# Layer 1's weight words bounded in a PSUM bank: clamp and shift there, the sign set before the add, the transposes moved into the scores' bank

## The chip, the cores and the metric

The kernel runs on one core of a Trainium2 chip. The metric is device time in microseconds (us) for one execution of the whole program, the median of three runs. One further execution is profiled: its trace gives the start and duration of the instructions on each engine. The engines are TensorE (PE in the rows), VectorE (DVE), ScalarE (ACT), GpSimd (POOL) and SyncE (SP, which issues the DMAs here).

## What is computed

Sparse attention feeds two feed-forward layers. All three parts are fp32.

```python
# attention: q, k, v are (4, 8, 576, 64); heads 0-3 local mask, heads 4-7 strided mask (stride 32)
scores = scale * np.matmul(q, k.transpose(0, 1, 3, 2))
scores = np.where(masks[None], scores, -1e9)
attn = np.exp(scores - np.max(scores, axis=-1, keepdims=True))
attn = attn / (np.sum(attn, axis=-1, keepdims=True) + 1e-09)
x = np.matmul(attn, v)                       # -> (2304 tokens, 512)
# layer 1: w_in (512, 2048), w_out (2048, 512)
h = x @ w_in
x = (h - np.tanh(h)) @ w_out
# layer 2: w_gate, w_val (512, 1536), w_out (1536, 512)
g = x @ w_gate
out = (g * (1.0 / (1.0 + np.exp(-g))) * (x @ w_val)) @ w_out
```

## The kernel before

TensorE multiplies in a split form: every fp32 operand is held as two reduced-precision halves, a head and a rest, and a product is three matmuls (head by head, head by rest, rest by head; `mm3`, L252 to L254).

The weights arrive as 64-bit words, and each must be turned into such a pair of halves. A `Piece` is 128 x 512 of them. Its steps are: `load` (a DMA into a slot `st` with a low and a high 32-bit word of each weight); `high` (ScalarE, the magnitude of the high word into `m`, L161); `low` (ScalarE, the low word scaled down, L164); the bounding of `m`, a clamp between two limits and a shift left and right that re-bases the exponent (VectorE); `join` (GpSimd, L189, adds the low word to `m`); `sign` (VectorE, L193, sets the sign bit of the high word into `m`); `head` (ScalarE, L199, the first half into `w`) and `rest` (GpSimd, L202, the second half).

Layer 1 has 32 such pieces, two for each slice `f` of 128 hidden columns. In the kernel before, `bound` does the clamp and the shift as two `scalar_tensor_tensor` instructions on `m` in place (L178 and L182). Their second input is a broadcast of a limit which lies in two spare columns of a PSUM bank (`limits`). One piece has the word `rebase` in its place: the two `tensor_scalar` forms of `clamp` and `shift` (L167 and L171), which work in SBUF alone. Layer 2's 36 pieces use `clamp`, `shift`, `join` and `sign` throughout.

Attention runs in groups of three blocks of scores. Its steps for a group are `scores` (TensorE, L344 or L352), `top` (VectorE, L360: mask, store to `s`, and the maximum of a row, three custom instructions with a read of the accumulator each), `exp` (ScalarE, L369), `recip` (VectorE, L382), `mult` (GpSimd, L387), `turn` (TensorE, L403: three transposes of `s` into PSUM), `bring` (VectorE, L407: a copy of them to SBUF as `pt`), `value` (TensorE, L415) and `keep` (ScalarE, L425, out of PSUM).

Two PSUM banks are set aside for this, `banks[0]` and `banks[1]`. Of `banks[0]` the scores take the first 288 columns and the values the rest; the transposes take 384 columns of `banks[1]`. The remaining banks hold the sums of layer 1.

What sets the order. There is no reordering on the chip: every engine takes its instructions in the order in which the program issues them. The first stretch, to about 60 us, is a text, `BEGIN`, that `Opening.run` reads word by word: `piece.3.bound` calls `bound` of piece 3, `turn.9` the transposes of group 9, `less.0`, `gh.0` and `gl.0` the three steps between the two products of layer 1's slice 0 (h - tanh h on VectorE, L824; the head on ScalarE, L828; the rest on VectorE, L833), `first` and `second` stretches of the two products (L798 and L811). After it a loop over `f` from 5 to 15 finishes the first chunk of 512 tokens. An iteration `f` there holds: the first product (12 matmuls, L252 to L254); `tanh` and `less` (ScalarE L608, VectorE L609; the function `bend`); the values of group f - 3 and the scores of group f; a `tick` of the weight feed; `top` of group f; the second product for f - 1 (12 matmuls, L628); `turn` and `bring` of group f - 1; the head and rest of f (ScalarE L615, VectorE L616; `parts`); `exp`, `recip`, `mult` of group f; and a second `tick`. Groups of this chunk end with group 16, and those of the loop then belong to the next batch. A tick issues `high` and `low` of one piece, `bound` and `join` of the piece before it and `sign`, `head` and `rest` of the one before that. Later chunks and layer 2 use no step of the change.

Of the kernel before, what the change touches and what calls it, by code (L numbers as in the profile page):

```python
# [70 lines left out]
piece.0.join piece.0.sign exp.7.c value.3 recip.6 piece.1.high mult.5.P low.2 turn.5 warm.12 keep.3 piece.1.low  # L71
bring.5.V words.2 ready.99.2 recip.7 top.8 exp.8.n mult.7.P warm.6 piece.1.bound value.4 keep.4 turn.7 keys.0.3
queries.0.3 mult.6.P bring.7.V turn.6 value.5 recip.8 piece.1.join piece.1.sign piece.0.head piece.2.high keep.5
scores.10 values.0.2 scores.9 scores.11 bring.6.V value.6 mult.8.P high.3 piece.0.rest ready.8.6 turn.8 low.3
piece.1.head words.3 xh.6 piece.1.rest top.9 top.10 exp.10.n values.0.3 xl.6 value.7 piece.2.bound words.4 words.5
keys.1.0 recip.10 top.11 ready.9.6 exp.9.c recip.9 mult.9.P xh.7 xl.7 piece.3.high mult.10.P ready.11.2 part.0.2
part.0.3 bring.8.V exp.11.c piece.3.low part.1.2 piece.3.bound recip.11 value.8 xh.8 left.8 xl.8 turn.9 turn.10
bring.9.V mult.11.A bring.10.V part.1.3 piece.3.join queries.1.0 value.9 values.1.0 keys.1.1 piece.2.low queries.1.1
piece.2.join xh.9 piece.4.high turn.11 piece.3.sign piece.3.head xl.9 part.0.0 bring.11.V value.10 value.11
piece.5.high xh.10 xh.11 piece.4.bound part.1.0 values.1.1 xl.11 left.11 first.3.2.1 xl.10 piece.4.low piece.5.low  # L80
words.6 scores.12 piece.2.sign piece.2.head piece.3.rest piece.5.bound half.0.0 half.0.1 words.7 piece.4.join tanh.0
top.12 piece.2.rest half.1.0 less.0 scores.13 half.1.1 first.3.2.11 piece.4.sign exp.12.c top.13 gh.0 gl.0
piece.5.join exp.13.c scores.14 second.2.0.8 tanh.1 piece.5.sign piece.5.head recip.12 recip.13 tanh.2 words.8 words.9
# [1675 lines left out]
```

## Time and profile before

| | |
|---|---|
| median of 3 runs | 865.82 us (865.76 to 866.29) |
| profiled execution | 866.21 us, of which the span of the trace is 864.4 us |
| granted TensorE clock | 1.00 throughout |
| TensorE busy | 859.2 us, 99% of the span |
| VectorE busy | 639.5 us, 74% |
| ScalarE busy | 463.8 us, 54% |
| GpSimd busy | 335.1 us, 39% |

The trace has a row for each instruction or run of equal instructions: start, duration, engine, source line, operation, output and inputs. Matmuls overlap in the pipeline, so that the durations of neighbours on TensorE add up to more than the time between them; distances between starts are what counts there. VectorE, too, starts an instruction some 0.1 us before the one ahead is recorded as ended. From the page's slices, VectorE is busy for over 90% of the time from about 22 to 130 us, where the weights of layer 1 are prepared, and less in most of the rest.

### The profile page before, as it was taken

To read this page: it belongs to the slowest core of one execution; us is meant where nothing else is said; L and a number is where in the kernel's file an instruction comes from. 1 tells how busy PE (TensorE), PEld (TensorE's weight loads), DVE (VectorE), ACT (ScalarE), POOL (GpSimd) and SP (SyncE) were. 2 spreads that over 40 slices of the span, in tenths; PEclk is the share of its full clock that TensorE was granted. 3 is DMA by queue.
4 is the path that set the end of the run, shared out by engine and by line. 5 is a ranking of instruction groups with operands and counts; after the bars stand their busy time and mean duration, and the time that the engine had idled before them with its cause. 6 is when DMAs were issued, how large, how long until landed. Compare 5 with 4: busy or idle time off the path is not lost.

```text
span 864.4 us, 13937 instructions
## 1 busy us (share of the span) xinstructions
PE 859.2 (99%) x4791; PEld 721.1 (83%) x4791; DVE 639.5 (74%) x1219; ACT 463.8 (54%) x1059; POOL 335.1 (39%) x284
## 2 busy tenths in 40 slices
PE   9999999999999999999999999999999999999998
PEld 7877778888888889998888888888888888888887
DVE  6999996688867786247887887788777867785461
ACT  6988874534343524237644655655454446854531
POOL 3889994754546550004125214463553310000000
PEclk9999999999999999999999999999999999999999
DMA  9867646530452213247456436453445469978651
GB/s 278 285 233 243 198 164 206 208 98 25 129 191 89 75 50 122 98 151 248 138 171 216 149 120 198 146 196 140 163 160 170 160 202 313 369 239 288 194 190 43
DMA packets 67398, 152.49 MB, mean 176 GB/s; under 512 B 7616, under 2 KB 14400, under 8 KB 67328
## 3 DMA queue, kind: packets, MB, share of 16 engines
q1 hardware_dynamic: 66752, 151.19, 52.2%
q8 instruction: 38, 0.62, 0.3%
q10 hardware_dynamic: 576, 0.41, 0.2%
q14 instruction: 32, 0.26, 0.1%
HBM read 108.06 MB, written 43.52 MB: 175 GB/s over the span
## 4 chain that ended last, share of the span: by engine, by line
PE 91%; DVE 4%; ACT 3%; issue 1%; DMA 0%; POOL 0%; SPq 0%; POOLq 0%
PE ps_acc L628 18%; PE ps_h L253 8%; PE ps_h L252 8%; PE ps_h L254 8%; PE ps_acc L252 8%; PE ps_acc L254 8%; PE ps_acc L253 8%; PE ps_a L252 5%; PE ps_a L253 5%; PE ps_a L254 5%; DVE m L193 2%; PE ps_acc L1628 2%; PE ps_a L415 1%; PE ps_a L344 1%; ACT s L369 1%
## 5 line engine op out<-in xcount | busy, mean ns | idle before, releaser
L628 PE MATMUL ps_acc<-gh,w 128*128 128x512 f32 (+1 forms) x546 | 124.8, 370 | 0.0
L189 POOL TENSOR_TENSOR sl<-sl,st 128x512 int32<-128x512 int32 x36 | 51.5, 1436 | 165.0 <-DVE sl L171 139.8
L252 PE MATMUL ps_acc<-sl 128*128 128x512 f32 x288 | 112.1, 389 | 0.0
L253 PE MATMUL ps_acc<-sl 128*128 128x512 f32 x288 | 112.1, 389 | 0.0
L254 PE MATMUL ps_acc<-sl 128*128 128x512 f32 x288 | 112.0, 389 | 0.0
L628 PEld LDWEIGHTS ps_acc<-gh,w 128*128 128x128 f32 x546 | 94.1, 189 | 16.1
L1214 DVE TENSOR_TENSOR sl<-sl 128x512 fp32r<-128x512 f32 (+1 forms) x120 | 71.8, 660 | 22.9 <-ACT sl L1210 22.8
L252 PE MATMUL ps_h<-xh,w 128*128 128x512 f32 (+1 forms) x226 | 85.0, 376 | 0.0
L253 PE MATMUL ps_h<-xh,w 128*128 128x512 f32 (+1 forms) x226 | 84.5, 374 | 0.1
L254 PE MATMUL ps_h<-xl,w 128*128 128x512 f32 (+1 forms) x226 | 84.2, 372 | 0.0
L1210 ACT CAST sl<-sl 128x512 fp32r<-128x512 f32 (+1 forms) x120 | 66.3, 602 | 24.7 <-DMA sl<-gd 18.8
L608 ACT ACTIVATE t<-ps_h 128x512 f32<-128x512 f32 (+1 forms) x54 | 30.5, 564 | 82.8 <-PE ps_h L254 82.8
L467 POOL TENSOR_TENSOR pr<-skv,sq 128x576 f32<-128x576 f32 (+8 forms) x40 | 57.5, 1463 | 44.4 <-DVE sc L474 31.1
L628 PE MATMUL ps_acc<-gl,w 128*128 128x512 f32 (+1 forms) x273 | 67.1, 366 | 0.0
L609 DVE TENSOR_TENSOR ps_h<-ps_h,t 128x512 f32<-128x512 f32 (+1 forms) x54 | 35.5, 658 | 41.0 <-ACT t L608 40.7
L254 PEld LDWEIGHTS ps_acc<-sl 128*128 128x128 f32 x288 | 54.1, 188 | 11.3
L252 PEld LDWEIGHTS ps_acc<-sl 128*128 128x128 f32 x288 | 54.1, 188 | 11.1
L253 PEld LDWEIGHTS ps_acc<-sl 128*128 128x128 f32 x288 | 54.1, 188 | 11.0
L467 POOL TENSOR_TENSOR pr<-skv,sc 128x576 f32<-128x576 f32 (+8 forms) x40 | 45.9, 1164 | 37.7 <-DVE xo L474 28.1
L252 PE MATMUL ps_a<-sl 128*128 128x512 f32 x144 | 56.1, 390 | 0.0
L253 PE MATMUL ps_a<-sl 128*128 128x512 f32 x144 | 56.1, 390 | 0.0
L254 PE MATMUL ps_a<-sl 128*128 128x512 f32 x144 | 56.0, 389 | 0.0
(211 smaller groups left out, 2098.4 us busy)
## 6 DMA issues: line engine op xcount, KB each, us to landing
st<-in_w SPq DMA_DIRECT2D x68, 512.0 KB, 4.4
gd<-t SPq DMA_DIRECT2D x84, 256.0 KB, 2.2
sl<-gd SPq DMA_DIRECT2D x84, 256.0 KB, 4.9
w<-w1s SPq DMA_DIRECT2D x32, 512.0 KB, 3.5
w3s<-sl SPq DMA_DIRECT2D x24, 256.0 KB, 3.3
sl<-w3s SPq DMA_DIRECT2D x24, 256.0 KB, 5.3
x2d<-o SPq DMA_DIRECT2D x17, 256.0 KB, 2.7
w1s<-w SPq DMA_DIRECT2D x8, 512.0 KB, 5.3
```

Of the source, the lines that this page charges most:

```text
L189: nc.gpsimd.tensor_tensor(out=mi, in0=mi, in1=self.lo, op=ALU.add)
L193: nc.vector.scalar_tensor_tensor(out=mi, in0=self.hi, scalar=-2 ** 30, in1=mi, op0=ALU.bitwise_and, op1=ALU.bitwise_or,)
L252: nc.tensor.matmul(ps, lhsT=wh, rhs=xh, start=start, stop=False, skip_group_check=goes_on)
L253: nc.tensor.matmul(ps, lhsT=wl, rhs=xh, start=False, stop=False, skip_group_check=goes_on)
L254: nc.tensor.matmul(ps, lhsT=wh, rhs=xl, start=False, stop=stop, skip_group_check=goes_on)
L467: nc.gpsimd.tensor_tensor(out=t, in0=x, in1=y, op=ALU.mult)
L608: nc.scalar.activation(t[:, :n], ps[:, :n], AF.Tanh)
L609: nc.vector.tensor_tensor(out=ps[:, :n], in0=ps[:, :n], in1=t[:, :n], op=ALU.subtract)
L628: nc.tensor.matmul(acc[m][:, :n], lhsT=w[:, i, m * P:(m + 1) * P], rhs=(gl if low else gh)[:, :n], start=start and not low and i == 0, sto ...
L1210: nc.scalar.copy(got[0][:, 0, :n], got[0][:, 1, :n].bitcast(F32))
L1214: nc.vector.tensor_tensor(out=w[:, 1, :n], in0=w[:, 1, :n].bitcast(F32), in1=w[:, 0, :n].bitcast(F32), op=ALU.subtract)
L1628: nc.tensor.matmul(ps[:, :c1 - c0], lhsT=lhsT, rhs=w[:, i, c0:c1], start=u == first and lhsT is zh and i == 0, stop=u == last and lhsT is zl)
```

## The change

`bound` becomes three instructions. The clamp is a `tensor_scalar` from `m` in SBUF into `banks[1]`, which now belongs to VectorE alone and is called `bounded`. The shift is a `tensor_scalar` in place in that bank. The third, a `scalar_tensor_tensor`, takes the sign bit of the high word from the slot and joins it to the shifted bits from PSUM, and writes `m`. The step `sign` goes out of layer 1's pieces; GpSimd's `join` then adds the low word to a word that has its sign already. The word `rebase` and the limits with their two memsets go. The transposes (`turned`) move to the first 384 columns of `banks[0]`, over the columns of the scores and the first 96 of the values, so that one bank now holds scores, transposes and values in turn. In the text `BEGIN` the words `sign` are dropped, `keep.12`, `keep.13`, `turn.14` and `bring.14` stand earlier, and nothing else is moved.

```diff
-    scored, valued, turned = banks[0][:, :GB * W_LOC], banks[0][:, GB * W_LOC:], banks[1][:, :GB * P]
-    limits = banks[1][:, 504:506]
+    scored, valued, turned = banks[0][:, :GB * W_LOC], banks[0][:, GB * W_LOC:], banks[0][:, :GB * P]
+    bounded = banks[1]
...
-        def rebase(self):
-            self.clamp()
-            self.shift()
-
         def bound(self):
+            bits = bounded.bitcast(I32)
+            nc.vector.tensor_scalar(bounded, self.m, HI_LEAST, HI_MOST, ALU.max, ALU.min)
+            nc.vector.tensor_scalar(bits, bits, 5, 2, ALU.logical_shift_left, ALU.logical_shift_right)
             nc.vector.scalar_tensor_tensor(
-                out=self.m, in0=self.m, scalar=HI_LEAST, in1=limits[:, 0:1].to_broadcast([P, 512]), op0=ALU.max, op1=ALU.min,
-            )
-            mi = self.m.bitcast(I32)
-            nc.vector.scalar_tensor_tensor(
-                out=mi, in0=mi, scalar=5, in1=limits.bitcast(I32)[:, 1:2].to_broadcast([P, 512]),
-                op0=ALU.logical_shift_left, op1=ALU.logical_shift_right,
+                out=self.m.bitcast(I32), in0=self.hi, scalar=-2 ** 30, in1=bits, op0=ALU.bitwise_and, op1=ALU.bitwise_or,
             )
...
-        def tick(self, hold=False, bound="bound"):
+        def tick(self, hold=False):
...
             if t - 1 >= self.since:
-                self.do(t - 1, bound, "join")
+                self.do(t - 1, "bound", "join")
             if t - 2 >= self.since - 1:
-                self.do(t - 2, "sign")
                 self.held = t - 2
...
-        nc.vector.memset(limits[:, 0:1], HI_MOST)
-        nc.vector.memset(limits.bitcast(I32)[:, 1:2], 2)
```

Of the text, one stretch (words around the moved ones):

```diff
-piece.7.sign second.4.1.4 piece.6.rest recip.15 piece.8.join bring.13.V piece.9.bound second.6.2.8 piece.8.sign
-keep.12 value.13 piece.7.head keys.1.2 queries.1.2 piece.7.rest piece.10.high mult.15.P piece.9.low scores.16
+second.4.1.4 piece.6.rest recip.15 piece.8.join bring.13.V turn.14 piece.9.bound second.6.2.8 bring.14.V value.13
+piece.7.head keys.1.2 queries.1.2 piece.7.rest piece.10.high mult.15.P piece.9.low scores.16 piece.9.join less.3
```

In the rows that follow, each instruction stands in its engine's order, with the kind of engine or queue that it waits for in brackets; lines are those of the kernel that the rows are from. `ps_a_91` is `banks[0]` and `ps_a_92` is `banks[1]`.

VectorE in the opening, from the copy `bring.8` (the first COPY) over piece 3 to `bring.11` (the last), before:

```order
L407 COPY pt<-ps_acc 96x384
L178 SCALAR_TENSOR_TENSOR m<-m,ps_a_92 128x512 [waits Activation_49]
L182 SCALAR_TENSOR_TENSOR m<-m,ps_a_92 128x512 [waits DVE_49]
L382 RECIPROCAL sm<-sm 128x3 [waits Activation_49]
L762 TENSOR_TENSOR xl<-ps_a_91,xh 128x128 [waits PE_49,Activation_49]
L407 COPY pt<-ps_acc 96x384 [waits PE_49] x2
L193 SCALAR_TENSOR_TENSOR m<-st,m 128x512 [waits DMAHW4_49,Pool_49]
L762 TENSOR_TENSOR xl<-ps_a_91,xh 128x192 [waits Activation_49]
L407 COPY pt<-ps_acc 96x384 [waits DVE_49,PE_49]
```

and now (L173 to L175 are the new `bound`, L398 is `bring`):

```order
L398 COPY pt<-ps_acc 96x384
L173 TENSOR_SCALAR ps_a_92<-m 128x512 [waits Activation_49]
L174 TENSOR_SCALAR ps_a_92<-ps_a_92 128x512 [waits DVE_49]
L175 SCALAR_TENSOR_TENSOR m<-st,ps_a_92 128x512 [waits DMAHW4_49,DVE_49]
L373 RECIPROCAL sm<-sm 128x3 [waits Activation_49]
L751 TENSOR_TENSOR xl<-ps_a_91,xh 128x128 [waits PE_49,Activation_49]
L398 COPY pt<-ps_acc 96x384 [waits PE_49] x2
L751 TENSOR_TENSOR xl<-ps_a_91,xh 128x192 [waits Activation_49]
L398 COPY pt<-ps_acc 96x384 [waits DVE_49,PE_49]
```

Three instructions stand between `bring.8` and the copies `bring.9` and `bring.10` where there were two, and the one of the sign between `bring.10` and `bring.11` is gone.

VectorE in the loop, from `less` (L609, now L600) over a piece's bounding to the first instruction of `top` (ISA), before:

```order
L609 TENSOR_TENSOR ps_h<-ps_h,t 128x512 [waits Activation_49]
L178 SCALAR_TENSOR_TENSOR m<-m,ps_a_92 128x512
L182 SCALAR_TENSOR_TENSOR m<-m,ps_a_92 128x512 [waits DVE_49]
L193 SCALAR_TENSOR_TENSOR m<-st,m 128x512 [waits DMAHW4_49,Pool_49]
L360 ISA s,mx<-ps_a_91,mask_l 128x96 [waits Activation_49]
```

and now:

```order
L600 TENSOR_TENSOR ps_h<-ps_h,t 128x512 [waits Activation_49]
L173 TENSOR_SCALAR ps_a_92<-m 128x512 [waits DVE_49]
L174 TENSOR_SCALAR ps_a_92<-ps_a_92 128x512 [waits DVE_49]
L175 SCALAR_TENSOR_TENSOR m<-st,ps_a_92 128x512 [waits DMAHW5_49,DVE_49,Pool_49]
L351 ISA s,mx<-ps_a_91,mask_l 128x96 [waits Activation_49]
```

The three instructions between `less` and `top` stay three, but the third belongs to the same piece as the two ahead of it and waits for the second of them; it was the sign of the piece before, and waited for GpSimd's `join`.

TensorE from `value.12` (L415, now L406) over `scores.15`, `turn.13` and the second product to `value.13`, before:

```order
L415 MATMUL ps_a_91<-pt,vt 64x64 [waits DMAHW2_49,DVE_49]
L415 MATMUL ps_a_91<-pt,vt 64x64 x5
L352 MATMUL ps_a_91<-kt,qt 64x80 [waits DMAHW4_49,DMAHW3_49]
L352 MATMUL ps_a_91<-kt,qt 64x80 x5
L403 MATMUL ps_a_92<-ident_sb,s 80x128 [waits DVE_49]
L403 MATMUL ps_a_92<-ident_sb,s 80x128 x2
L811 MATMUL ps_h<-gh,w_826 128x512 [waits Pool_49]
L811 MATMUL ps_acc<-gh,w_826 128x512 x6
L811 MATMUL ps_h<-gl,w_826 128x512
L811 MATMUL ps_acc<-gl,w_826 128x512 x3
L811 MATMUL ps_h<-gh,w_900 128x512 [waits Activation_49]
L811 MATMUL ps_h<-gh,w_900 128x512 [waits Pool_49]
```

and now:

```order
L406 MATMUL ps_a_91<-pt,vt 64x64 [waits DMAHW2_49,DVE_49]
L406 MATMUL ps_a_91<-pt,vt 64x64 x5
L343 MATMUL ps_a_91<-kt,qt 64x80 [waits DMAHW4_49,DMAHW3_49]
L343 MATMUL ps_a_91<-kt,qt 64x80 x5
L394 MATMUL ps_a_91<-ident_sb,s 80x128 [waits Activation_49]
L394 MATMUL ps_a_91<-ident_sb,s 80x128 x2
L800 MATMUL ps_h<-gh,w_824 128x512 [waits Pool_49]
L800 MATMUL ps_acc<-gh,w_824 128x512 x6
L800 MATMUL ps_h<-gl,w_824 128x512
L800 MATMUL ps_acc<-gl,w_824 128x512 x3
L394 MATMUL ps_a_91<-ident_sb,s 80x128 [waits DVE_49,Pool_49]
L394 MATMUL ps_a_91<-ident_sb,s 80x128 x2
```

`turn.13` (L403, now L394) writes the bank that `scores.15` has just filled and waits for ScalarE besides what it needs; `turn.14` now stands behind the first products of `second`, ahead of `value.13` and of `scores.16`; before, it came behind `scores.16`. In the loop no instruction of TensorE changes its place, but there too the transposes of group f - 1 now write the bank that the scores of group f have filled: they wait for `top` of group f on VectorE and `keep` of group f - 3 on ScalarE, besides GpSimd's `mult`.

## Rows read from the trace of the kernel before

**Rows 1.** The page: busy time of each engine, share of the span, instructions.

```profile
PE 859.2 (99%) x4791; PEld 721.1 (83%) x4791; DVE 639.5 (74%) x1219; ACT 463.8 (54%) x1059; POOL 335.1 (39%) x284
```

**Rows 2.** Timeline, TensorE, iteration 8: start, duration, engine, line, operation, out<-in.

```profile
82.30 0.48 PE L252 MATMUL ps_acc<-xh,w 128*128 128x512 f32 x1
...
84.91 0.39 PE L254 MATMUL ps_acc<-xl,w 128*128 128x512 f32 x1
...
89.09 0.49 PE L403 MATMUL ps_a<-ident_sb,s 128*96 128x128 f32 x3
89.33 0.48 PE L252 MATMUL ps_h<-xh,w 128*128 128x512 f32 x1
```

**Rows 3.** Timeline, VectorE, the same iteration.

```profile
79.92 0.68 DVE L178 SCALAR_TENSOR_TENSOR m<-m,ps_a 128x512 f32<-128x512 f32 x1
80.63 0.69 DVE L182 SCALAR_TENSOR_TENSOR m<-m,ps_a 128x512 int32<-128x512 int32 x1
81.23 1.58 DVE L193 SCALAR_TENSOR_TENSOR m<-st,m 128x512 int32<-128x512 int32 x1
82.74 0.24 DVE L360 CUSTOM_DVE_ANT_0 s<-ps_a,mask_l 128x96 f32<-128x96 f32 x1
...
83.27 0.54 DVE L407 COPY pt<-ps_a 96x384 f32<-96x384 f32 x1
...
84.34 0.67 DVE L178 SCALAR_TENSOR_TENSOR m<-m,ps_a 128x512 f32<-128x512 f32 x1
...
85.65 0.69 DVE L193 SCALAR_TENSOR_TENSOR m<-st,m 128x512 int32<-128x512 int32 x1
...
86.45 0.70 DVE L609 TENSOR_TENSOR ps_acc<-ps_acc,t 128x512 f32<-128x512 f32 x1
```

**Rows 4.** Timeline, GpSimd, beside the long sign of rows 3.

```profile
80.97 1.30 POOL L202 TENSOR_TENSOR w<-m,w 128x512 fp32r<-128x512 f32 x1
```

**Rows 5.** VectorE by form: count | busy us, mean ns | idle before, releaser.

```profile
L193 DVE SCALAR_TENSOR_TENSOR m<-st,m 128x512 int32<-128x512 int32 x32 | 32.5, 1014 | 0.9 <-POOL m L189 0.8
...
L167 DVE TENSOR_SCALAR sl<-sl 128x512 f32<-128x512 f32 x36 | 20.5, 584 | 0.4 <-ACT sl L999 0.4
```

**Rows 6.** Timeline, all engines: the end of a first product and its `less`.

```profile
120.29 0.39 PE L254 MATMUL ps_h<-xl,w 128*128 128x512 f32 x1
...
121.35 0.70 DVE L609 TENSOR_TENSOR ps_h<-ps_h,t 128x512 f32<-128x512 f32 x1
```

**Rows 7.** Timeline, VectorE, the opening.

```profile
31.07 1.01 DVE L407 COPY pt<-ps_acc 96x384 f32<-96x384 f32 x2
...
37.28 0.23 DVE L360 CUSTOM_DVE_ANT_0 s<-ps_acc,mask_s 128x80 f32<-128x80 f32 x1
...
43.42 0.69 DVE L833 TENSOR_TENSOR gl<-ps_h,gh 128x512 fp32r<-128x512 f32 x1 [0.18 <-ACT gh L828]
44.03 1.30 DVE L167 TENSOR_SCALAR m<-m 128x512 f32<-128x512 f32 x1
45.37 0.43 DVE L171 TENSOR_SCALAR m<-m 128x512 int32<-128x512 int32 x1
...
48.48 0.24 DVE L360 CUSTOM_DVE_ANT_0 s<-ps_a,mask_s 128x80 f32<-128x80 f32 x1
...
51.57 0.53 DVE L407 COPY pt<-ps_a 80x384 f32<-80x384 f32 x1
```

**Rows 8.** Timeline, TensorE, the opening.

```profile
31.81 0.57 PE L415 MATMUL ps_a<-pt,vt 96*64 96x64 f32 x12
...
48.36 0.53 PE L403 MATMUL ps_a<-ident_sb,s 128*80 128x128 f32 x3
...
53.17 0.57 PE L415 MATMUL ps_a<-pt,vt 80*64 80x64 f32 x12
```

**Rows 9.** Timeline, TensorE, the longest gap between two starts in the loop.

```profile
117.33 0.48 PE L252 MATMUL ps_h<-xh,w 128*128 128x512 f32 x1
117.89 0.50 PE L253 MATMUL ps_h<-xh,w 128*128 128x512 f32 x1
```

More of the change, by code (lines that the diff above doesn't have):

```diff
@@ L70 @@
 bring.3.V turn.4 high.2 scores.6 bring.4.V recip.5 top.6 scores.7 values.0.1 words.1 top.7 scores.8 exp.6.n
[L71 to L83, printed above, removed]
+piece.0.join exp.7.c value.3 recip.6 piece.1.high mult.5.P low.2 turn.5 warm.12 keep.3 piece.1.low bring.5.V words.2
@@ new lines @@
+ready.99.2 recip.7 top.8 exp.8.n mult.7.P warm.6 piece.1.bound value.4 keep.4 turn.7 keys.0.3 queries.0.3 mult.6.P
+bring.7.V turn.6 value.5 recip.8 piece.1.join piece.0.head piece.2.high keep.5 scores.10 values.0.2 scores.9 scores.11
+bring.6.V value.6 mult.8.P high.3 piece.0.rest ready.8.6 turn.8 low.3 piece.1.head words.3 xh.6 piece.1.rest top.9
+top.10 exp.10.n values.0.3 xl.6 value.7 piece.2.bound words.4 words.5 keys.1.0 recip.10 top.11 ready.9.6 exp.9.c
+recip.9 mult.9.P xh.7 xl.7 piece.3.high mult.10.P ready.11.2 part.0.2 part.0.3 bring.8.V exp.11.c piece.3.low part.1.2
@@ new lines @@
+piece.3.bound recip.11 value.8 xh.8 left.8 xl.8 turn.9 turn.10 bring.9.V mult.11.A bring.10.V part.1.3 piece.3.join
+queries.1.0 value.9 values.1.0 keys.1.1 piece.2.low queries.1.1 piece.2.join xh.9 piece.4.high turn.11 piece.3.head
+xl.9 part.0.0 bring.11.V value.10 value.11 piece.5.high xh.10 xh.11 piece.4.bound part.1.0 values.1.1 xl.11 left.11
+first.3.2.1 xl.10 piece.4.low piece.5.low words.6 scores.12 piece.2.head piece.3.rest piece.5.bound half.0.0 half.0.1
+words.7 piece.4.join tanh.0 top.12 piece.2.rest half.1.0 less.0 scores.13 half.1.1 first.3.2.11 exp.12.c top.13 gh.0
@@ L84 @@
+gl.0 piece.5.join exp.13.c scores.14 second.2.0.8 tanh.1 piece.5.head recip.12 recip.13 tanh.2 words.8 words.9
 piece.4.head second.2.0.4 mult.12.P mult.13.P top.14 less.1 gh.1 second.4.1.1 less.2 piece.6.high gl.1 piece.5.rest
-piece.6.rebase turn.12 piece.4.rest exp.14.c piece.6.low bring.12.V piece.7.high piece.7.low first.5.3.12 recip.14
-piece.8.high piece.8.low piece.7.bound value.12 gh.2 scores.15 piece.6.join piece.6.sign piece.6.head top.15 exp.15.c
+piece.6.bound turn.12 piece.4.rest exp.14.c piece.6.low bring.12.V piece.7.high piece.7.low first.5.3.12 recip.14
@@ L87 @@
+piece.8.high piece.8.low piece.7.bound value.12 gh.2 scores.15 piece.6.join piece.6.head top.15 keep.12 exp.15.c
 piece.9.high gl.2 tanh.3 mult.14.P turn.13 second.4.1.7 piece.7.join words.10 words.11 spill.5 piece.8.bound
-piece.7.sign second.4.1.4 piece.6.rest recip.15 piece.8.join bring.13.V piece.9.bound second.6.2.8 piece.8.sign
-keep.12 value.13 piece.7.head keys.1.2 queries.1.2 piece.7.rest piece.10.high mult.15.P piece.9.low scores.16
-piece.9.join turn.14 less.3 second.6.2.4 bring.14.V top.16 words.12 gh.3 first.7.4.1 piece.10.bound keep.13
@@ new lines @@
+piece.7.head keys.1.2 queries.1.2 piece.7.rest piece.10.high mult.15.P piece.9.low scores.16 piece.9.join less.3
+second.6.2.4 top.16 keep.13 words.12 gh.3 first.7.4.1 piece.10.bound gl.3 first.7.4.11 turn.15 bring.15.V piece.8.head
+piece.8.rest piece.10.low words.13 second.8.3.1 piece.11.low piece.11.high tanh.4 second.8.3.11 piece.10.join
+piece.11.bound words.14 piece.9.head piece.9.rest spill.8 exp.16.c less.4 piece.12.high piece.10.head words.15 gh.4
+piece.11.join piece.13.high piece.13.low piece.10.rest piece.12.bound gl.4 piece.12.low piece.12.join
```

4 lines of the change are left out of this document (removed).

## The prediction

> **What bounds the kernel now.** I read the page first: TensorE is busy for 99% of the span, VectorE for 74% [rows 1]. So the whole runs at TensorE's pace, and a change on VectorE counts only where TensorE waits for VectorE. Then the timeline of TensorE and VectorE side by side, for one iteration of the loop in which the layer 1 weights are made. TensorE starts iteration 8 at 82.30 and the next at 89.33, a period of 7.03 us with matmul behind matmul [rows 2]. VectorE does not wait there either: `top` starts at 82.74, `bring` at 83.27, a bounding at 84.34, a sign at 85.65, the next `less` at 86.45 [rows 3]. Two engines have nearly the same period, and any work added to VectorE's comes out on TensorE.
>
> What that work holds is seen in the same rows. An instruction on 512 columns takes 0.60 us from its start to the next one's (81.23 - 80.63, 85.65 + 0.60 for the sign ahead of a 0.20 `recip`), and 0.71 where the next one reads what it wrote (79.92 to 80.63) [rows 3]. But one sign of the two in an iteration takes 1.58 instead of 0.69. It ends just after GpSimd's L202 does, which started at 80.97 for 1.30 and so ends at 82.27, and then takes its usual 0.6 more [rows 4]. Both read SBUF with all their inputs. Over the 32 pieces the signs take 32.5 us, 1014 ns each, against 0.69 for an undisturbed one [rows 3, 5]: about 10 us of blocked VectorE that the change could give back.
>
> The rule for it is in the Trainium skill, SBUF — State Buffer, section "Who interferes with whom": a VectorE instruction with two SBUF inputs and a GpSimd instruction that reads SBUF share a port pair as a lock, and one with a single SBUF input does not take part. By that rule the old clamp and shift were free of it (one input is in PSUM), the sign was not, and the new third instruction is; the 1.58 against 0.69 agrees.
>
> **The change part by part.** Signs removed: 32 instructions, 32.5 us of VectorE's busy time [rows 5], about 0.60 us of its time for an undisturbed one, 1.5 for a blocked one (82.74 - 81.23) [rows 3].
>
> Bound: two dependent instructions, 0.71 + 0.60 = 1.31 us (79.92 to 81.23) [rows 3], become three in a chain. No row shows a `tensor_scalar` that writes PSUM. The nearest from below is the one in SBUF, 0.43 us at 45.37 [rows 7]; from above the group L167, whose mean of 584 ns holds blocked ones, and a blocked case of 1.30 at 44.03 [rows 5, 7]; between them L178 and L182, with one operand in PSUM, 0.67 to 0.69 [rows 3]. I take the last: 0.71 + 0.71 + 0.61 = 2.03 us, 0.71 more than before per piece (rounding up). Both ends kept: 1.5 us if the clamp and shift run as in SBUF (two times 0.44, and 0.61), and 2.3 to 2.6 if reading back a bank just written is dearer than any row here.
>
> Against this change speaks the Trainium skill, VectorE: DVE Perf Modes, section "Why PSUM operands drop a tier": any PSUM operand brings fp32 down to one element a cycle. By it a bound of two fast SBUF instructions would be given up for two slow ones, as I take them; by the SBUF row instead the sum would be about nothing, the low end above.
>
> So VectorE gets less work in total, but another order of it. The sign stood two pieces late and nothing waited for it soon; now its time lies inside `bound`, ahead of `bring` and `top`, for which TensorE waits.
>
> *The opening.* Two bounds lie ahead of the copies `bring.9` and `bring.10` at 31.07 [rows 7] since VectorE last waited. They add 1.42, so the copies start at 32.49 and the first is done at about 33.0. TensorE began `value.9` at 31.81 [rows 8]: it is 1.2 late. Then VectorE loses two signs, at 0.60 or a little more, and gains two more bounds: 1.42 - 1.20 + 1.42 = 1.64 late at `top.12` (37.28) [rows 7]. After that VectorE loses two more signs, but it cannot use them: `exp.12` and then `gh.0`, `tanh.1` and `gh.1` on ScalarE follow that `top` in ScalarE's order, and `gl.1` already waited 0.18 for the last of them at 43.42 [rows 7]. I let 1.4 of the delay through: `gl.1` at 44.8, and the next bound at 45.4.
>
> That bound was the word `rebase`: 44.03 to 45.71 (45.37 + 0.34) for clamp and shift, the clamp at 1.30 blocked for 0.9 [rows 7]. The new one takes 2.03 and ends at 47.45, 1.74 late. Bound 7 adds 0.71, a sign goes with 0.60: `top.15` starts at 48.48 + 1.85 = 50.33 and ends 0.5 later [rows 7]. Here the shared bank matters. `turn.13` stood at 48.36 beside `top.15` [rows 8]; now it must not write before `top.15` has read the scores, and `keep.12` the values (on ScalarE, moved up; its wait is for `value.12`, some 2 us earlier). It starts at about 50.9: 2.5 late, 0.6 to 0.9 of it by the bank. Behind it on TensorE wait the products of `second`, and everything that follows. `bring.13` comes at 51.57 + 1.85 + 0.71 - 0.60 = 53.5 and ends at 54.05 [rows 7]; `turn.14`, now ahead of `value.13`, needs that copy done (same bank), and TensorE is there 0.2 before. `value.13` in turn must wait for `bring.14`, which now stands behind another bound: 54.05 + 2.03 + 0.5 = 56.6. Before, it came at 53.17 [rows 8] with `turn.14` still ahead, which takes 0.24 (89.09 to 89.33) [rows 2]: 56.6 - 53.17 - 0.24 = 3.2 late. The signs taken out here were some 0.1 longer than 0.60, so I say 3.0 for the opening. No DMA is held by it: SP's order is unchanged, and the words' slots come free at the joins, which wait for no sign any more. `keep.13`, moved up on ScalarE, waits for `value.13` ahead of some `high` and `low`; these are a tick early as they were.
>
> *The loop.* `less` starts 1.06 us after the last matmul of the first product does (120.29 to 121.35, where ScalarE was idle) [rows 6]. In iteration 8 that matmul is at 84.91, 2.61 after the start [rows 2], so `less` can be at 3.67. Then 0.61, the bound of 2.03, and `top` of 0.53 with its read: done at 6.9. TensorE reaches the transposes at 89.09 - 82.30 = 6.79 [rows 2], where until now nothing of `top` was needed. They wait 0.2. And a circle closes: transposes to `bring` 0.55 (an estimate: 0.49 and a handover), `bring` and `gl` 1.07 (84.34 - 83.27), bound 2.03, `recip` 0.20, `less` 0.61, bound 2.03, `top` 0.60, handover 0.05: 7.15 us against 7.03 [rows 2, 3]. Over the seven iterations with scores and `top` (5 to 11) that is 0.2 + 6 x 0.12 = 0.9, I say 1.1 with what the handovers hide. The blocked sign (0.9 an iteration) is already out of this circle; without that it would be 8.
>
> In return the loop's few stalls go, since the weights come sooner. They are seen only as distances: 117.33 to 117.89 is 0.56 for a matmul recorded at 0.48 whose neighbours overlap [rows 9]. This one is the longest, some 0.3; with four shorter ones ahead of it I take 0.8 and use it whole. After the loop TensorE has no step of the change to wait for, and it is full to the end, so what is lost stays lost.
>
> Sum: + 3.0 + 1.1 - 0.8 = 3.3 us. The profiled execution took 866.21, 0.39 above the median of 865.82; 866.21 + 3.3 = 869.5 in its terms, 869.1 in the median's.
>
> **Rivals.**
>
> 1. *Chained instructions cost no more than others.* The 0.10 between 0.60 and 0.71 is then absent in PSUM and bound is 1.82, 0.51 more. `value.9` is 0.8 late, `top.15` 0.5 late by the same steps, `turn.13` 1.1, `value.13` 1.3; the circle is 6.73, below 7.03, and the loop gains its 0.8. Sum + 0.5: 866.3. For it: between instructions that do not read each other the gap is absent (80.63 to 81.23). Against: the writer and its reader at 79.92 and 80.63 have it [rows 3]. A sentence of the Trainium skill goes this way (VectorE: DVE Perf Modes, section "The DRAIN you can't avoid"): a semaphore between two such instructions costs nothing extra; the 0.71 disagrees.
>
> 2. *Not slower: the bound is short.* Clamp and shift run near SBUF's 0.43, bound is at most 1.5, and with the signs' blocked time gone VectorE is ahead of TensorE at every `top` and `bring`. The place is `top.15`: below a bound of about 1.6 it ends before TensorE comes to `turn.13`. Then only the stalls change: 865.82 - 0.8 = 865.0. For it: 10 us less blocked time. Against: nothing with an operand in PSUM and 512 columns takes under 0.67 in any row [rows 3, 5].
>
> 3. *VectorE becomes the bound of the loop.* If the bank's read behind its write costs 0.15 more at each of two places, bound is 2.3 and the circle 7.7: 7 x 0.67 = 4.7 in the loop and about 4 in the opening, less 0.8: near 874. No row speaks for it but that none excludes it.
>
> **How the numbers follow.** Forecast 0.62 (its own range 867.6 to 871.2: the handovers, and whether ScalarE passes on the opening's delay whole), rival 1 0.18, rival 2 0.12, rival 3 0.08. The range reaches from 865.4, near rival 2, to 871.5 and leaves rival 3 and half of rival 2 out. A measurement of this kernel tells 0.2%, 1.7 us, from no change. Faster by that would need TensorE to find 1.7 us, and all its gaps that depend on this work come to about 1: 0.03. Within it lie rivals 1 and 2 nearly whole: 0.28. Slower is the forecast and rival 3: 0.69.
>
> **What would show it.** The three rows of the new bound start 0.71, 0.71 and 0.61 apart, and the third never takes 1.5. `value.9` starts near 33.0, `turn.13` near 50.9 right behind `top.15`, `value.13` near 56.5 behind `bring.14`. Iterations 5 to 11 are 7.1 to 7.2 apart, with the transposes released by VectorE. Wrong I would be if TensorE's rows after 61 us stood less than 1 us later than before, or if a shift in PSUM took 0.45.

## The result, and the profile after

The changed kernel takes 872.71 us (median of 4 runs, 871.76 to 873.56) against 865.82; the ratio is 1.0078, 95% interval 1.0061 to 1.0096. It is slower, as forecast, but by 6.9 us and not by 3.3, and outside the range. The profiled execution has a span of 870.2 us, 5.8 more than before. The last matmul of TensorE starts 6.06 us later than before. The remaining 0.8 to 1.1 us of the median lies outside the span: in four runs of the changed kernel the time exceeded the span by 2.1 to 3.4 us, where it was 1.7 to 2.0 in the runs of the kernel before. What it is, the trace cannot show. Single runs of other kernels have it too (2.8 us once in e10_control), and e3_keep, the changed kernel with two words moved, has 1.8 to 1.9 in all its runs, so that it need not belong to the change. It stays open, and the rest of this text is on the 6 us that TensorE loses.

The page's line of busy times answers to [rows 1]: VectorE and GpSimd have less to do, TensorE the same work in a longer span.

```profile
PE 861.0 (99%) x4791; PEld 720.7 (83%) x4791; DVE 632.2 (73%) x1217; ACT 463.0 (53%) x1059; POOL 324.1 (37%) x284
```

The groups of the bounding by form (count, busy us, mean ns, idle before), which answer to [rows 5]. Each of the three instructions takes its 0.67 to 0.70 and none is ever blocked: 66 us for 32 pieces, where clamp, shift and sign took 76 with the blocked signs (the `rebase` of [rows 7] included).

```profile
L174 DVE TENSOR_SCALAR ps_a<-ps_a 128x512 int32<-128x512 int32 x32 | 22.4, 699 | 1.1
L175 DVE SCALAR_TENSOR_TENSOR m<-st,ps_a 128x512 int32<-128x512 int32 x32 | 22.0, 689 | 2.9 <-DVE ps_a L174 0.4
L173 DVE TENSOR_SCALAR ps_a<-m 128x512 f32<-128x512 f32 x32 | 21.8, 682 | 0.0
```

So the instructions last what was forecast; what they take from start to start is in the rows further down. TensorE's waits tell where the time went (engine, output, line, releaser, us in total, times, longest). L394 are the transposes, L406 the values. The view has four more lines of 0.2 to 1.1 us, two of which were there before. Two of the lines shown name an engine that was not waited for: `value.9` (L406, 0.8) is put down to ScalarE's L385, but the copy that it reads ends at 33.1, just ahead of it; and the six waits of L394 are put down to the exponential L360, which the transposes do not need, while `top` ends 0.15 ahead of them (rows below).

```profile
PE ps_a L394 <- ACT x L416: 1.7, 1, 1.7
PE ps_a L394 <- ACT s L360: 1.6, 6, 0.6
...
PE ps_a L406 <- ACT s L385: 0.8, 1, 0.8
```

In the opening, the rows of TensorE that answer to [rows 8], then VectorE's that answer to [rows 7] (L751 is the rest `xl` of an attention output, L822 is `gl`):

```profile
33.24 0.57 PE L406 MATMUL ps_a<-pt,vt 96*64 96x64 f32 x12 [0.78 <-ACT s L385]
...
51.95 0.53 PE L394 MATMUL ps_a<-ident_sb,s 128*80 128x128 f32 x3 [1.67 <-ACT x L416]
...
57.30 0.57 PE L406 MATMUL ps_a<-pt,vt 80*64 80x64 f32 x12
```

```profile
32.60 1.01 DVE L398 COPY pt<-ps_acc 96x384 f32<-96x384 f32 x2
34.25 0.36 DVE L751 TENSOR_TENSOR xl<-ps_a,xh 128x192 fp32r<-128x192 f32 x1 [0.64 <-ACT xh L747]
...
39.68 0.23 DVE L351 CUSTOM_DVE_ANT_0 s<-ps_acc,mask_s 128x80 f32<-128x80 f32 x1
...
45.61 0.69 DVE L822 TENSOR_TENSOR gl<-ps_h,gh 128x512 fp32r<-128x512 f32 x1 [0.30 <-ACT gh L817]
...
50.92 0.23 DVE L351 CUSTOM_DVE_ANT_0 s<-ps_a,mask_s 128x80 f32<-128x80 f32 x1
```

`value.9` is 1.43 late (1.2 forecast), `turn.13` 3.59 (2.5), `value.13` 57.30 - 53.17 - 0.25 = 3.9 (3.2 forecast, of which I took 3.0; the 0.25 is `turn.14`, which now stands ahead of it). `turn.13` is put down to ScalarE's `keep.12`, which itself waited for `top.15`:

```profile
51.58 0.32 ACT L416 COPY x<-ps_a 128x192 f32<-128x192 f32 x1 [0.35 <-DVE mx L351]
```

In the loop, iteration 8 starts at 87.12 and the next at 94.53: 7.41 us, where 7.03 was in [rows 2]. The circle of the prediction can be read row by row, from one set of transposes to the next. TensorE, with the last matmul of the first product (L245), then ScalarE's `tanh` (L599), then VectorE (answering to [rows 3]; L607 is `gl`, L373 `recip`, L600 `less`):

```profile
86.86 0.50 PE L394 MATMUL ps_a<-ident_sb,s 128*96 128x128 f32 x3 [0.20 <-ACT s L360]
87.12 0.48 PE L243 MATMUL ps_acc<-xh,w 128*128 128x512 f32 x1
...
89.73 0.39 PE L245 MATMUL ps_acc<-xl,w 128*128 128x512 f32 x1
...
94.27 0.51 PE L394 MATMUL ps_a<-ident_sb,s 128*96 128x128 f32 x3 [0.20 <-ACT s L360]
94.53 0.47 PE L243 MATMUL ps_h<-xh,w 128*128 128x512 f32 x1
```

```profile
90.16 0.60 ACT L599 ACTIVATE t<-ps_acc 128x512 f32<-128x512 f32 x1 [1.21 <-PE ps_acc L245]
```

```profile
87.41 0.55 DVE L398 COPY pt<-ps_a 96x384 f32<-96x384 f32 x1 [0.69 <-PE ps_a L394]
87.88 0.68 DVE L607 TENSOR_TENSOR gl<-ps_h,gh 128x512 fp32r<-128x512 f32 x1
88.48 0.68 DVE L173 TENSOR_SCALAR ps_a<-m 128x512 f32<-128x512 f32 x1
89.19 0.70 DVE L174 TENSOR_SCALAR ps_a<-ps_a 128x512 int32<-128x512 int32 x1
89.98 0.69 DVE L175 SCALAR_TENSOR_TENSOR m<-st,ps_a 128x512 int32<-128x512 int32 x1
90.59 0.17 DVE L373 RECIPROCAL sm<-sm 128x3 f32<-128x3 f32 x1
90.79 0.70 DVE L600 TENSOR_TENSOR ps_acc<-ps_acc,t 128x512 f32<-128x512 f32 x1
91.40 0.68 DVE L173 TENSOR_SCALAR ps_a<-m 128x512 f32<-128x512 f32 x1
92.12 0.70 DVE L174 TENSOR_SCALAR ps_a<-ps_a 128x512 int32<-128x512 int32 x1
92.91 0.69 DVE L175 SCALAR_TENSOR_TENSOR m<-st,ps_a 128x512 int32<-128x512 int32 x1
93.51 0.25 DVE L351 CUSTOM_DVE_ANT_0 s<-ps_a,mask_l 128x96 f32<-128x96 f32 x1
...
94.04 0.08 DVE L351 DVE_READ_ACCUMULATOR2_ANT mx<- 128x1 f32 x1
```

Transposes to `bring` 0.55, `bring` and `gl` 1.07, bound 2.11 (88.48 to 90.59), `recip` 0.20, `less` 0.61, bound 2.11 (91.40 to 93.51), `top` with its last read 0.61, and 0.15 to the transposes: 7.41.

But a second circle of the same length runs beside it, through TensorE's own first product, and the rows say that this one sets the pace. Transposes to the first product 0.26 (86.86 to 87.12), 2.61 to its last matmul, 0.43 to `tanh`, 0.63 to `less`, 0.61, bound 2.11, `top` 0.61, and 0.15: 7.41. `tanh` waited 1.21 for that product, and `less` starts 0.63 after `tanh` in each of the iterations 5 to 12. In VectorE's own circle the 0.20 behind `recip` is then partly a wait for ScalarE: in e5_ahead, where `less` comes 0.95 us or more after `tanh` and does not depend on its end, `less` follows `recip` by 0.08 to 0.09. Without that wait VectorE's circle would be 7.3. So of the two bounds only the one between `less` and `top` is on the path, and the one ahead of `less` has about 0.1 us to spare.

TensorE's lateness, by the starts of iterations against the kernel before: 3.86 us at iteration 5 (65.09 against 61.23), 6.58 at iteration 12, 6.07 at iteration 14, and 6.06 at iteration 15 as at the last matmul. So the opening costs 3.9, the loop 2.7, and 0.5 comes back in iterations 12 and 13, where the kernel before had its stalls.

### The profile page after: what moved, and what is told of

It is laid out like the page before. It is cut to its first block, busy times and chain, and to the rows that moved or that the text cites. A ratio compares the mean times of both kernels' runs of the same rounds, so it can differ in the third digit from the quotient of the medians.

```text
span 870.2 us, 13938 instructions
## 1 busy us (share of the span) xinstructions
PE 861.0 (99%) x4791; PEld 720.7 (83%) x4791; DVE 632.2 (73%) x1217; ACT 463.0 (53%) x1059; POOL 324.1 (37%) x284
## 3 DMA queue, kind: packets, MB, share of 16 engines
q1 hardware_dynamic: 66752, 151.19, 51.6%
## 4 chain that ended last, share of the span: by engine, by line
PE 91%; DVE 5%; ACT 3%; issue 1%; DVEq 0%; POOL 0%; POOLq 0%
PE ps_acc L619 18%; PE ps_h L243 8%; PE ps_acc L244 8%; PE ps_acc L243 8%; PE ps_h L245 8%; PE ps_h L244 8%; PE ps_acc L245 8%; PE ps_a L244 5%; PE ps_a L243 5%; PE ps_a L245 5%; PE ps_acc L1617 2%; DVE ps_a L174 1%; PE ps_a L406 1%; DVE ps_a L173 1%; DVE m L175 1%; PE ps_a L335 1%
## 5 line engine op out<-in xcount | busy, mean ns | idle before, releaser
L245 PE MATMUL ps_acc<-sl 128*128 128x512 f32 x288 | 112.0, 389 | 0.0
L245 PE MATMUL ps_h<-xl,w 128*128 128x512 f32 (+1 forms) x226 | 84.3, 373 | 0.0
L599 ACT ACTIVATE t<-ps_h 128x512 f32<-128x512 f32 (+1 forms) x54 | 30.5, 565 | 89.8 <-PE ps_h L245 89.7
L600 DVE TENSOR_TENSOR ps_h<-ps_h,t 128x512 f32<-128x512 f32 (+1 forms) x54 | 35.5, 658 | 42.5 <-ACT t L599 42.2
L245 PEld LDWEIGHTS ps_acc<-sl 128*128 128x128 f32 x288 | 54.1, 188 | 11.3
L245 PE MATMUL ps_a<-sl 128*128 128x512 f32 x144 | 56.0, 389 | 0.0
```

The costliest lines, as they stand in the source:

```text
L245: nc.tensor.matmul(ps, lhsT=wh, rhs=xl, start=False, stop=stop, skip_group_check=goes_on)
L599: nc.scalar.activation(t[:, :n], ps[:, :n], AF.Tanh)
L600: nc.vector.tensor_tensor(out=ps[:, :n], in0=ps[:, :n], in1=t[:, :n], op=ALU.subtract)
```

## The experiments

Theory A: TensorE waits because the shared bank puts the transposes behind `top` and `keep`, in the opening once and in the loop in a circle. Theory B: the longer bounding with the sign ahead of `bring` and `top` costs, and the bank is harmless. Theory C is for the opening alone: its loss is not a sum of single waits, each to be taken out by another order, but VectorE's longer bounding and the engines' load. One caution for all of them: the executions do not reach the opening at the same time. The first matmul of `mm3` starts at 27.58 us before, at 27.74 in the change, and between 27.11 and 28.45 in the others. Counted from it, iteration 5 is as late as before to within 0.02 us in the three kernels with the old opening (e8, e10, e11), and 3.7 late in the change.

**The bank alone (e1_bank).** The kernel before, with old bound and late sign:

```diff
-    scored, valued, turned = banks[0][:, :GB * W_LOC], banks[0][:, GB * W_LOC:], banks[1][:, :GB * P]
+    scored, valued, turned = banks[0][:, :GB * W_LOC], banks[0][:, GB * W_LOC:], banks[0][:, :GB * P]
     BEGIN: keep.12, keep.13, turn.14 and bring.14 moved as in the change
```

> The kernel before with one part of the change: the transposes write the scores' bank, with the words keep.12, keep.13, turn.14 and bring.14 moved as in the change; clamp, shift and the late sign stay as before. Theory A (the shared bank ties TensorE's transposes to top, and the loop becomes a circle transposes - bring - gl - bound - less - bound - top - transposes that holds all VectorE work): the circle is here 0.55 + 1.07 + 1.31 + 0.60 + 0.20 + 0.61 + 1.31 + 1.5 + 0.60 + 0.2 = 7.95 us against 7.03, 0.9 for each of seven iterations, and about 1 in the opening: 872 to 874 us, iterations 5 to 11 some 7.9 apart. Theory B (the loss is the longer work of the new bound and sign ahead of bring and top; where the transposes go is harmless): 865.5 to 866.5 us.

873.37 us, ratio 1.0084 (1.0067 to 1.0101). Iterations 6 to 11 are 7.80 to 7.89 apart (7.95 forecast). The third instruction between `less` and `top` is the late sign, blocked in the row shown, 1.35 long, and TensorE waits some 0.7 at each set of transposes. `less` waits 0.23 for ScalarE here, so this circle, too, runs through the first product. Here are the rows of `less` and of the sign, and that of the transposes behind them:

```profile
90.79 0.70 DVE L609 TENSOR_TENSOR ps_acc<-ps_acc,t 128x512 f32<-128x512 f32 x1 [0.23 <-ACT t L608]
...
92.72 1.35 DVE L193 SCALAR_TENSOR_TENSOR m<-st,m 128x512 int32<-128x512 int32 x1
```

```profile
94.75 0.51 PE L403 MATMUL ps_a<-ident_sb,s 128*96 128x128 f32 x3 [0.68 <-ACT w L199]
```

The bank alone costs as much as the whole change: theory B falls, at least as a full account. But the loss stands elsewhere: 5.7 us of it in the loop, where the blocked sign is now on the path, and 1.6 in the opening (63.73 - 61.23, less the 0.87 by which this execution is late at the first `mm3`). The change has 2.7 and 3.7. So e1 does not show that the bank is what the change's opening pays for.

**The sign ahead alone (e5_ahead).** The kernel before, the transposes in their own bank:

```diff
         def bound(self):
             ...
+            self.sign()
...
-                self.do(t - 2, "sign")
     BEGIN: the words sign dropped, piece.6.rebase now piece.6.bound
```

> The kernel before with the other part of the change: the sign is set right behind the shift and ahead of GpSimd's add, as a third instruction of bound, but all three work in place on m in SBUF as the old ones did, and the transposes keep a bank of their own. The third still has two SBUF inputs. Theory A: the opening loses what the bounds ahead of bring and top cost, 1.2 to 2.5 us at value.12, but not the wait of the transposes for top; the loop holds no circle and its iterations stay within 7.0 to 7.2: 867.5 to 869.5 us. Theory B: the order of the work is what costs, so most of the change's loss is here: 871 to 873 us.

875.06 us, ratio 1.0104 (1.0089 to 1.0119): the slowest of all, against both theories as I had written them. The sign has two SBUF inputs here and stands on the path now. It is blocked more than before: 1088 ns in the mean ([rows 5] had 1014 off the path).

```profile
L192 DVE SCALAR_TENSOR_TENSOR m<-st,m 128x512 int32<-128x512 int32 x32 | 34.8, 1088 | 1.1
```

Iteration 5 is 5.2 us late (some of it the lower clock, last section), and the loop's iterations are 7.1 to 7.5 apart without a shared bank: TensorE waits for the rest of a piece (L201 on GpSimd) in the first product. So the two parts do not add up: the bank alone costs as much as the change (7.3 and 6.9 us, with overlapping intervals), and the sign alone costs more (9.0). With the sign ahead, the PSUM bank is worth having, since its third instruction is not blocked; without, it only ties the transposes.

**`top` first (e2_top).** The changed kernel with one line moved in the loop:

```diff
                 if c == 0:
                     ...
+                    if f in gs:
+                        gs[f].top()
                     feed1.tick(True)
...
-                if f in gs:
+                if f in gs and c > 0:
                     gs[f].top()
```

> The changed kernel with top of group f issued ahead of the loop's first tick, so that VectorE does it before the bounding; opening and bank as in the change. Theory A: top ends 0.61 + 0.6 after less starts, about 4.9 us into the iteration, and the transposes at 6.8 wait for nothing; iterations 5 to 11 come 7.0 to 7.1 apart instead of 7.4, and TensorE's lateness stays near the 3.9 us of iteration 5: about 869.5 to 870.5 us. Theory B: VectorE's work in an iteration is the same in sum, so its order changes little: 872 to 873 us.

870.04 us, ratio 1.0047 (1.0032 to 1.0062). Iterations 7 to 11 are 7.03 apart again. `top` follows `less` at once, the bound comes behind it while TensorE is still in the second product, and the transposes wait for nothing; `bring` follows them:

```profile
90.76 0.70 DVE L600 TENSOR_TENSOR ps_acc<-ps_acc,t 128x512 f32<-128x512 f32 x1
91.49 0.26 DVE L351 CUSTOM_DVE_ANT_0 s<-ps_a,mask_l 128x96 f32<-128x96 f32 x1
...
92.03 0.69 DVE L173 TENSOR_SCALAR ps_a<-m 128x512 f32<-128x512 f32 x1
...
94.41 0.55 DVE L398 COPY pt<-ps_a 96x384 f32<-96x384 f32 x1 [0.18 <-PE ps_a L394]
```

```profile
93.89 0.49 PE L394 MATMUL ps_a<-ident_sb,s 128*96 128x128 f32 x3
```

VectorE does the same instructions; only their place in the circle differs: the bound is no longer between `less` and `top`. Theory A stands for the loop.

**The loop alone (e11_looponly, e8_loop) and a control (e10_control).** Opening as before; new bound and shared bank from the loop on; e8 with `top` first, e11 with `top` where the change has it; e10 is the kernel before with `top` first and nothing else.

```diff
+        def signed(self):    # the new bound, in banks[1]
...
-        def tick(self, hold=False, bound="bound"):
+        def tick(self, hold=False, bound="signed"):
...
-                self.do(t - 2, "sign")
+                if t - 2 < AT - 1:
+                    self.do(t - 2, "sign")
...
-                        gs[f - 1].turn(turned, "a")
+                        gs[f - 1].turn(banks[0][:, :GB * P], "a")
```

> The kernel of e8_loop with top behind the first tick, as in the change: opening as before, the change in the loop alone. Theory A: the circle of 7.4 us is back in iterations 5 to 11, which makes TensorE some 2 to 2.7 us late at 131 us: 867.5 to 869 us, and with the opening's loss of e2_top (3.9 us) it adds up to the whole change. If the loop loses only because the opening hands it over late, this is as e8_loop, 866 to 866.7 us.

> The kernel before with the change in the loop alone: opening, its bounds, late signs and bank for the transposes as before; from the loop on the new bound in PSUM (pieces 13 to 31), transposes in the scores' bank, and top issued ahead of the first tick. Theory A: no loss in the opening, iterations 7.03 us apart with the few stalls of the kernel before gone: 865.0 to 865.8 us, TensorE 0 to 0.8 us earlier than before at 131 us. Theory C (new bound and shared bank cost wherever they stand): 1 to 3 us slower than before.

> The kernel before with one thing moved: top of group f ahead of the loop's first tick, as in e2_top and e8_loop; everything else as before. It is the control of e8_loop. If the tie of e8_loop is the new bound's own, this is 865.5 to 866.5 us, as the kernel before, or slower where a blocked sign now falls ahead of bring. If it was the moved top that paid for a slower bound there, this is 0.5 to 1 us faster than before.

e11: 868.78 us, ratio 1.0027 (1.0018 to 1.0037); iterations 6 to 11 are 7.39 to 7.41 apart, iteration 5 takes 8.39. e8: 866.71, ratio 1.0000 (0.9991 to 1.0009); 6.93 to 7.05 apart but for two of 7.37 and 7.16. e10: 865.55, ratio 0.9990 (0.9981 to 0.9998), 7.01 to 7.18 apart. TensorE's first transposes of the loop in e11:

```profile
69.15 0.50 PE L413 MATMUL ps_a<-ident_sb,s 128*80 128x128 f32 x3 [1.28 <-DVE mx L370]
69.40 0.48 PE L262 MATMUL ps_acc<-xh,w 128*128 128x512 f32 x1
...
76.55 0.50 PE L413 MATMUL ps_a<-ident_sb,s 128*80 128x128 f32 x3 [0.21 <-ACT s L379]
76.81 0.47 PE L262 MATMUL ps_h<-xh,w 128*128 128x512 f32 x1
```

The circle comes from the change in the loop, without the opening's lateness. With `top` first the new bound ties with the kernel before, but the moved `top` pays for part of that: the control, which has the same move with the old bound, takes 1.2 us less than e8 in the median (single runs 865.4 to 866.56 against 865.67 to 867.7), and it is the only kernel here whose interval lies below 1, with 0.1%. Why e8 has two long iterations is not shown. In the control the signs of 61 to 131 us take 794 ns in the mean instead of 1052, and `less` waits for ScalarE again, 2.9 us in all: the moved `top` shifts the sign from under GpSimd's L202. That row of the control, then the one of before for the same stretch:

```profile
L193 DVE SCALAR_TENSOR_TENSOR m<-st,m 128x512 int32<-128x512 int32 x22 | 17.5, 794 | 0.6 <-POOL m L189 0.6
```

```profile
L193 DVE SCALAR_TENSOR_TENSOR m<-st,m 128x512 int32<-128x512 int32 x21 | 22.1, 1052 | 0.0
```

**The opening (e3_keep, e6_fill, e7_early, e9_late5).** All by words of `BEGIN` alone; the last three have `top` first.

```diff
 e3_keep:  keep.12 ahead of top.15, keep.13 ahead of top.16
 e6_fill:  value.12 gh.2 keep.12 scores.15 ... second.4.1.7 turn.13 ... second.6.2.8 turn.14 ...
           less.3 gh.3 second.6.2.4 bring.14.V value.13 piece.9.bound ... scores.16 keep.13 top.16
 e7_early: e6_fill, piece.2.bound behind xh.11, piece.4.bound behind piece.2.join, piece.5.bound behind top.13
 e9_late5: e7_early, scores.15 keep.12 (was keep.12 scores.15), gl.0 piece.5.bound (was piece.5.bound gl.0)
```

> The changed kernel with two words of the opening moved: keep.12 ahead of top.15 and keep.13 ahead of top.16, so that ScalarE's copies of the values do not wait for VectorE's reading of the same bank. Theory A, with the wait of keep.12 as a part of the opening's loss: turn.13 starts about 0.45 us earlier, gh.3 about 1.4 us earlier, and iteration 5 comes 0.4 to 1.0 us earlier: 871.7 to 872.3 us. Theory B: the keeps are off the path: no difference from the change, 872.7 us.

873.40 us, ratio 1.0092 (1.0067 to 1.0116): no gain. `turn.13` came at 52.05 instead of 51.95. ScalarE reaches `keep.12` only at 50.88, and now `top.15` waits for it:

```profile
51.34 0.24 DVE L351 CUSTOM_DVE_ANT_0 s<-ps_a,mask_s 128x80 f32<-128x80 f32 x1 [0.55 <-ACT x L416]
```

> The kernel of e2_top (changed kernel, top first in the loop) with TensorE's words from value.12 to turn.15 in another order: second.4.1.7 ahead of turn.13, second.6.2.8 ahead of turn.14, second.6.2.4 ahead of value.13; keep.12 right behind gh.2, bring.14 ahead of piece 9's bound. Theory A (in the opening TensorE stands still because transposes and values wait in line for the shared bank): the gap of 1.7 us ahead of turn.13 is filled with products, iteration 5 comes near 63, 1.5 to 2 us late instead of 3.9 to 5.0, the loop keeps 7.03: 867 to 868 us. Theory C (the opening's loss is VectorE's longer bounding as such, wherever TensorE's products stand): iteration 5 stays 3 us or more late, 869.5 to 870.5 us.

868.99 us, ratio 1.0032 (1.0020 to 1.0045). Iteration 5 is 3.1 us late instead of 3.9, but counted from the first `mm3` 3.4 instead of 3.7: the gap of 1.7 ahead of `turn.13` is gone, and only 0.3 is gained, since a new gap of 1.0 stands at `scores.15`, which waits for `keep.12`.

> The kernel of e6_fill with piece 2's bound moved behind the copies bring.9 to bring.11, and pieces 4's and 5's bounds behind what they delayed (piece 5's behind top.13). Theory A: value.9 is reached without the 0.8 to 1.2 us wait for VectorE's copy, iteration 5 comes 0.2 to 0.8 us late: 865.3 to 866.5 us. Theory C: the amount of bounding in the opening is as before, so the lateness comes back at a later place: 867 to 868 us, as e6_fill.

869.63 us, ratio 1.0036 (1.0022 to 1.0049). `value.9` is on time (31.71), but iteration 5 is 3.3 us late (3.4 from the first `mm3`, as in e6): the lateness is back at `second.2.0.8`, which waited for `gl.0`, and at `scores.15`:

```profile
PE ps_h L800 <- DVE gl L822: 1.1, 1, 1.1
PE ps_a L343 <- ACT x L416: 1.1, 1, 1.1
```

> The kernel of e7_early with two words moved: keep.12 behind scores.15 (in e6_fill and e7_early scores.15 waited 1.0 us for it) and gl.0 ahead of piece 5's bound (second.2.0.8 waited 1.1 us for it). Theory A (the opening's loss is the sum of single waits of TensorE, each to be taken out by order): both gaps go, iteration 5 comes 1 to 1.5 us late instead of 3.3: 867 to 868 us. Theory C (VectorE and ScalarE are full in the opening, so that what is moved out of one wait is late at the next): iteration 5 stays 2.5 us or more late, 868.5 to 869.5 us.

871.06 us, ratio 1.0052 (1.0038 to 1.0065): worse, with iteration 5 5.3 us late (4.6 from the first `mm3`; some of it is the lower clock, last section). Both gaps went, and one of 2.4 came: piece 5's bound is later, so GpSimd's `join` is, so ScalarE's `head.5` waits 2.4 in its order with `tanh.2` and `gh.1` behind it, and TensorE stands before `second.4.1.1`:

```profile
47.30 0.80 PE L800 MATMUL ps_h<-gh,w 128*128 128x512 f32 x1 [2.42 <-ACT gh L817]
```

```profile
45.13 0.62 ACT L191 CAST w<-m 128x512 fp32r<-128x512 f32 x1 [2.42 <-POOL m L181]
```

So theory A holds in the opening only as far as the gap at `turn.13`; for the rest iteration 5 stayed 3 us late or more in each of the three, as theory C has it, and the totals came out between the two theories (e6) or slower than both (e7, e9). Theory C's reason, the engines' load, does not follow from that. From 30 to 61 us VectorE is busy less in the change than before; the kernel before, then the change (busy us of PE, PEld, DVE, ACT, POOL, then clock, DMA share, GB/s):

```profile
30.00:61.00 31.00, 31.00 (x239) 25.54 (x238) 29.99 (x80) 27.99 (x82) 25.90 (x22) 1.00 0.77 254
```

```profile
30.00:61.00 31.00, 28.11 (x222) 22.54 (x222) 27.48 (x78) 24.95 (x75) 21.85 (x21) 1.00 0.78 259
```

Here VectorE has 3.5 us of idle time in the 31, and 3.9 to 5.0 in e6, e7 and e9. What the orders show is that a delay taken out of one wait came back at another. None of the four brought iteration 5 nearer than 3.1 us. That no order can is not shown, and how the opening's 3.9 us divide between the bank and the longer bound stays open: with the bank alone (e1) `value.12` is not late, and `turn.13` is by 1.15, both counted from `value.8`. The new bound in PSUM with the transposes in a bank of their own was not run.

## Why the prediction was off

*Right:* that it is slower and by what. The first and last price of the bound (0.71 and 0.61 forecast; 0.70 to 0.73 and 0.60 to 0.61 measured), the unblocked third instruction, the chain `value.9` - `top.15` - `turn.13` - `value.13`, the wait of the transposes for `top`, and a circle that this closes are in the rows in the order that was forecast. Rivals 1 and 2 fall with the rows of the bound, which takes 2.04 to 2.12 where nothing is waited for, and not 1.82 or 1.5. Rival 3 came nearer than its 0.08: a bound of 2.11 in the loop and a circle of 7.41 lie between the forecast's 2.03 and 7.15 and its 2.3 and 7.7, and the loop's 2.7 us between 1.1 and 4.7.

*The step that failed is the size of the circle.* I had 7.15 us, 0.12 above TensorE's period; it measured 7.41, 0.38 above. I had added up the circle through VectorE, with two bounds in it. The path that sets the pace, through the first product, was in the prediction as well, but its wait of 0.2 was counted once; a set of transposes that starts late makes the next product, `tanh` and `less` late, so it comes back in each iteration. At the prediction's own prices this circle is 0.24 + 3.67 + 0.61 + 2.03 + 0.53 + 0.05 = 7.13. It measured 0.26 + 3.67 + 0.61 + 2.11 + 0.61 + 0.15 = 7.41. Too small were the handover from `top` to the transposes by 0.10, `top` with its last read by 0.08, and the bound by 0.08: its third instruction starts 0.79 after the second where it waits for a DMA, VectorE and GpSimd, and 0.73 where it waits for two of these (31.00 to 31.73). With seven iterations and one hiccup of 0.3 (the third instruction at 100.66) that is 2.7 instead of 1.1. Two periods within 2% of each other should not have been given one value: 0.1 us of error in a few terms decided between 0 and 0.4 an iteration.

*The opening was mis-sized by 0.9.* `top.12` is 2.4 late (39.68 against 37.28; 1.64 forecast), because `value.9`'s own lateness came back: VectorE waited 0.64 at 34.25 for ScalarE's `xh.9`, which reads what `value.9` writes. That step was left out. I then let 1.4 through ScalarE; `gl.1` is at 45.61, 2.2 late, so nearly all came through, and the two signs that fell away behind `top.12` gave nothing, as was said. And `keep.12`, costed at nothing because its data is there early, waited for `top.15` by 0.35 (its row above), because it reads the bank that `top.15` reads and stands behind it in the program; e3 shows that in the other order the wait moves to `top.15`.

*The cover was 0.5, not 0.8:* the stalls of the kernel before in iterations 12 and 13 are gone (6.58 to 6.07 late). Together the three misses are 0.9 + 1.6 + 0.3 = 2.8, which is TensorE's 6.1 against the forecast's 3.3; the other 0.8 of the median is the part outside the span.

*What I did not see* is that the bank alone costs as much (e1) and that the order of one VectorE step in the loop undoes the loop's part (e2, e8). The circle was in the prediction; that it can be cut by putting `top` ahead of the bound was not. One reading was loose: the long sign of [rows 3] ends at 82.81, 0.54 after GpSimd's L202 does, and not just behind it.

## What to carry to other kernels

When two uses share a PSUM bank, write down the circles of waits that this closes, engine by engine and also through the busy engine itself, and add up the steps of each: if a sum is near the busy engine's period, each handover counts and the sum needs a range of its own. Then look at which step of the circle does not need to be in it, and issue that one late; here one moved line took away 2.1 (e11 to e8) to 2.7 us (the change to e2). Where several engines hand work to each other in turn, a freed instruction, or a wait taken out by another order, is no gain when the next step waits for another engine anyway.
